# One load for the small inputs, and a new order for the first batch's attention, in a fused attention and squared-ReLU kernel

## The chip, the core and the metric

The kernel runs on one core of a Trainium2 chip. The metric is the device time of one execution in microseconds (us); of the kernel before there are three runs of 1002.27, 1003.53 and 1003.83, median 1003.53. The engines are PE (TensorE, matrix products; its weight loads are a row of their own, PEld), DVE (VectorE), ACT (ScalarE), POOL (GpSimd) and SP (SyncE, which here only issues transfers). A transfer (DMA) can also be issued by ACT.

## What is computed

Eight batches of attention with 12 heads, 448 tokens and 64 columns a head, whose output feeds a two-matrix network with a gate:

```python
q_n, k_n = rmsnorm(q, g_q), rmsnorm(k, g_k)         # over the 64 columns
attn = softmax(q_n @ k_n.T / 8)                     # 448 x 448 a head
x = (attn @ v) put side by side over the heads      # 448 x 768 a batch
xk = mu_k * x + (1 - mu_k) * x_prev                 # x_prev: the token before
xr = mu_r * x + (1 - mu_r) * x_prev
k2 = maximum(xk @ w_k, 0) ** 2                      # w_k 768 x 1024
out = sigmoid(xr @ w_r) * (k2 @ w_v)                # w_r 768 x 768, w_v 1024 x 768
```

g_q and g_k have 64 numbers each, mu_k and mu_r 768 each.

## The kernel before

**Who sets the order.** The program is a set of Python generators (`setup`, `load`, `stats`, `preps`, `vpreps`, `scores`, `attends`, `mixk`, `wload`, `weights`, `moe` and more), each of which yields its next instruction. A planner (`Plan.run`) keeps an estimated clock for each engine and always emits the instruction with the smallest key: the time at which it could start, less a priority times `PS` = 0.1, so that a priority of 700 is worth 70 ns. The order emitted is fixed when the program is built; on the chip each engine works through its own list from the top, and an instruction that waits holds up everything behind it on that engine. Nearly all instructions are emitted in one helper line, L289 in the profile (L290 in the changed kernel), so groups are told apart by the tiles that they write and read.

**Attention.** Two heads are a pair, two pairs a quad; a batch has six pairs, three quads and 21 score groups. For the first batch (quads 0 to 2, `u < U32`) everything is in float32: q and k are scaled (`nat<-qk,ss`), turned by PE transposes (`ps<-ident,nat`), copied to `stk`, and multiplied (`ps<-stk`, 448 columns, one matmul a head and group). DVE takes the row maxima (`sums<-ps`), ACT the exponential with its row sums (`xk<-ps,sums` or `nat<-ps,sums`), POOL divides, PE turns the result back (`ps<-ident,nat` or `ps<-ident,xk`; `xk` here is only memory that is lent out), and DVE or ACT copies it to `pT`. That last part is the function `probs_pe`. When all groups of a pair are there, `attends` multiplies by v (`ps<-pT,vf`, 16 matmuls) and writes the pair's columns of x. From the second batch on the numbers are split into a high and a low half of 16 bits: three products a score group (`ps<-stk` in f16), the exponentials in place (`ps<-ps,sums`), the split (`nat<-ps,sums`), transposes by DMA (`pT<-nat`), and 22 matmuls for a pair's product with v (`ps<-pT,vh` and `ps<-pT,vl`).

**The network.** For each batch `mixk` builds xk from x: per 128 columns one ACT instruction (`ps<-x,bsc`), one on DVE (`df<-x,bsc,ps`), an ACT cast (`xk<-df`) and a POOL subtraction (`xk<-df,xk`); six such pieces make a batch. Then `moe` multiplies: 144 matmuls `ps<-xk,wk`, then 126 `ps<-wr,xr` and 168 `ps<-wv,kk` in turns, and ACT applies the gate (`o<-ps,bsc`). The gate's scale (`bsc`) needs the scales of all weights (`WIN`), so all weights must have been split first.

**Weights.** They arrive as 64-bit numbers in pieces (`raw`, `kk`), are reduced to 32 bits by POOL, ACT (`ps<-raw`) and DVE (`wk<-ps,wk`, and the like), squared and summed on PE (`ps<-wk`, `ps<-wr`, `ps<-wv`, bf16), and split in two halves on ACT and DVE or POOL. Their priority grows with the planner's time against `W_GAP` for each finished piece.

**The small inputs.** `setup` loads g_q and g_k by two transfers from SP that spread one row over 128 partitions. DVE then makes one scaled vector of them and a handful of factors (`gm`, `gc`), some 16 tiny instructions that depend on each other; every scaling of q and k needs `gm`. `mu_stats` loads mu_k and mu_r by two transfers from ACT, once the second quad is being loaded and a piece of weights is there; each puts 768 numbers of 4 bytes on 128 partitions, six a partition, one by one. DVE computes 1 - mu and the largest factor from them.

The lines that set the order here are, in `scores` and `probs_pe`:

```python
yield from until(lambda: u in TQ and len(banks["sc"].free) > (SC_KEEP if u < U32 or gi in PE_P else 1) and not st["zq"])
```

`TQ` holds the quads whose q and k are turned, and `banks["sc"].free` counts the PSUM banks that score groups may still take. Nothing else keeps the second batch's score groups back.

Of the kernel before, what the change touches and what calls it, by code (L numbers as in the profile page):

```python
# [7 lines left out]
F32 = mybir.dt.float32  # L8
# [8 lines left out]
P = 128  # L17
HD = 64
NT = 7
# [3 lines left out]
ND = D_MODEL // P  # L23
# [40 lines left out]
PRIO_M = 400  # L64
BOOST_K = 500
BOOST_R = 500
BOOST_A = 0
BOOST_W = 300
BOOST_Q = 600
SLACK_S = 3  # L70
# [8 lines left out]
Q_DVE = 1  # L79
V_POOL = True  # L80
PE_T = 6
U32 = 3
V_SIDE = 2
SWITCH = 600
# [7 lines left out]
LEAD_V = 1  # L92
LEAD_W = 1
PE_P = range(1, 21, 2)
SC_KEEP = 2
TR_COST = 130
W_GAP = 7e3
W_PUSH = 0.03
NEWTON_ON = "DVE"
OP_SLOW = 1.0  # L100
# [353 lines left out]
            yield V.scalar_tensor_tensor(out=y, in0=t, scalar=1.5, in1=y, op0=ALU.add, op1=ALU.mult)  # L454


def attn_moe_kernel(tc, q, k, v, g_q, g_k, mu_k, mu_r, w_k, w_v, w_r, out):
    nc = tc.nc
    B, H = 2 * out.shape[0], D_MODEL // HD
    NP = H // 2  # L460
# [1 line left out]
    const = ctx.enter_context(tc.tile_pool(name="const", bufs=1))  # L462
    small = ctx.enter_context(tc.tile_pool(name="small", bufs=3))
# [7 lines left out]
    T, V, A, G_, SP = (Engine(n, e) for n, e in (("PE", nc.tensor), ("DVE", nc.vector), ("ACT", nc.scalar), ("POOL", nc.gpsimd), ("SP", nc.sync)))  # L471
# [1 line left out]
    banks = {n: Share(psum, *c) for n, c in (("sc", SC_SHARE), ("mm", MM_SHARE), ("ot", OT_SHARE), ("wz", WZ_SHARE), ("pg", PG_SHARE), ("df", DF_SHARE))}  # L473

    ident16 = const.tile([P, P], BF16, name="ident16")
    gq = const.tile([P, HD], F32, name="gq")
    gk = const.tile([P, HD], F32, name="gk")
    mu = const.tile([P, 2, 2, ND], F32, name="mu")
    gm = const.tile([P, 8], F32, name="gm")
    G = gq  # L480
    gc = const.tile([P, 1], F32, name="gc")
# [14 lines left out]
    NQ, NPAIR, NSS, NSL, NVB = len(quads), len(pairs), 4 * NT, (NT + 1) // 2, 2 * NT  # L496
    VFREE = [const.tile([P, NVB, HD], F32, name="vf%d" % n) for n in range(VF_BUFS)]

    st = {"wdone": 0, "g": 0, "moe": 0, "vl": 0, "gm": False, "mus": False, "want": "xk", "sg": 0, "su": 0, "pu": 0, "vi": 0, "wkeys": 0, "kdone": 0, "zq": 0, "tq": 0, "lu": 0}
    LD, SS, VF, VV, TQ, PT, BS, BSC, XT, XK, XKN, XR, CNT, OS, CARRY, FR = {}, {}, {}, {}, {}, {}, {}, {}, {}, {}, {}, {}, {}, {}, {}, {}  # L500

    plan.st = st
# [1 line left out]
    def until(f):  # L504
        while not f():
            yield f
# [33 lines left out]
    for name, plan_ in (("kk", KK_LENT), ("xk", XK_LENT)):  # L540
        for _ in R[name].get():
            pass
        t = HOME[name] = next(iter(R[name].of.values()))[2]
        w = t.rearrange("p a b c -> p (a b c)")
# [20 lines left out]
    ring_sum = [small.tile([P, 12], F32, name="sums%d" % n, bufs=1) for n in range(6)]  # L565

    def setup():
        yield SP.dma_start(out=gq, in_=g_q.partition_broadcast(P))
        yield SP.dma_start(out=gk, in_=g_k.partition_broadcast(P))
        yield A.copy(out=ident16, in_=ident)  # L570
        yield V.memset(out=ones, value=1.0)
        st["vf"] = True
        yield V.scalar_tensor_tensor(out=G, in0=gq, scalar=1.0 / float(HD) ** 0.5, in1=gk, op0=ALU.mult, op1=ALU.mult)
        yield V.tensor_reduce(out=gm[:, 0:1], in_=G, axis=AX.X, op=ALU.max, apply_absolute_value=True)
        yield V.tensor_scalar(out=gm[:, 0:1], in0=gm[:, 0:1], scalar1=TINY, scalar2=None, op0=ALU.max)
        yield from rsqrt(V, gm[:, 1:2], gm[:, 0:1], gm[:, 5:6])
        yield V.tensor_scalar(out=G, in0=G, scalar1=gm[:, 1:2], scalar2=None, op0=ALU.mult)
        for h in range(2):
            hs = slice(h * HD, (h + 1) * HD)
            yield V.tensor_tensor(out=gd[hs, :], in0=G[hs, :], in1=ident[hs, hs], op=ALU.mult)  # L580
        yield V.tensor_reduce(out=gc, in_=gd, axis=AX.X, op=ALU.add)
        yield V.tensor_tensor(out=gm[:, 2:3], in0=gm[:, 1:2], in1=gm[:, 1:2], op=ALU.mult)
        yield V.tensor_scalar(out=gm[:, 3:4], in0=gm[:, 2:3], scalar1=1.0 / HD, scalar2=None, op0=ALU.mult)
        yield V.tensor_scalar(out=gm[:, 4:5], in0=gm[:, 2:3], scalar1=1e-6, scalar2=None, op0=ALU.mult)
        st["gm"] = True

    def mu_stats():
        yield from until(lambda: st["lu"] >= 1 and len(RAW))
        yield A.dma_start(out=mu[:, 0, 0, :], in_=mu_k.rearrange("(t p) -> p t", p=P))
        yield A.dma_start(out=mu[:, 1, 0, :], in_=mu_r.rearrange("(t p) -> p t", p=P))  # L590
        yield V.tensor_scalar(out=mu[:, :, 1, :], in0=mu[:, :, 0, :], scalar1=-1.0, scalar2=1.0, op0=ALU.mult, op1=ALU.add)
        u = small.tile([P, 2, ND], F32, name="muu")
        u2 = small.tile([P, 2, ND], F32, name="muu2")
        col = small.tile([P, 2], F32, name="mucol")
        yield V.tensor_scalar(out=u, in0=mu[:, :, 0, :], scalar1=2.0, scalar2=-1.0, op0=ALU.mult, op1=ALU.add)
        yield V.tensor_scalar(out=u2, in0=u, scalar1=-1.0, scalar2=1.0, op0=ALU.mult, op1=ALU.max)
        yield V.tensor_tensor(out=u, in0=u, in1=u2, op=ALU.max)
        yield V.tensor_reduce(out=col, in_=u, axis=AX.X, op=ALU.max)
        pt = yield from banks["ot"].get()
        yield T.transpose(form=("f", 200), out=pt[0:2, 0:P], in_=col, identity=ident)  # L600
        m = small.tile([P, 1], F32, name="allmax")
        yield V.tensor_reduce(out=m[0:2, :], in_=pt[0:2, 0:P], axis=AX.X, op=ALU.max)
        yield T.matmul(form=("f", 400), out=pt[:, P:P + 2], lhsT=m[0:2, :].broadcast_to([2, P]), rhs=ident[0:2, 0:2], start=True, stop=True)
        yield V.tensor_copy(out=smu, in_=pt[:, P:P + 2])
        banks["ot"].put(pt)
        yield V.reciprocal(out=ismu, in_=smu)
        st["mus"] = True
# [191 lines left out]

    def scores():  # L800
        for gi, (u, x, t0) in enumerate(groups):
            yield from until(lambda: u in TQ and len(banks["sc"].free) > (SC_KEEP if u < U32 or gi in PE_P else 1) and not st["zq"])
            tp = None
            if u < U32 or gi in PE_P:
# [77 lines left out]
    def probs_pe(u, x, t0, sums, tp):  # L882
# [8 lines left out]
        for a0 in range(0, NT, 4):  # L891
            m = min(4, NT - a0)
            st["zq"] += 1
            z = yield from banks["sc"].get()
            st["zq"] -= 1
            yield [T.transpose(form=("tr", TR_COST * m), out=z[:, a * P:(a + 1) * P], in_=tf[:, (a0 + a) * P:(a0 + a + 1) * P], identity=ident) for a in range(m)]
            src = z[:, 0:m * P].rearrange("p (a c) -> p a c", c=P)
            if u < U32:
                dst = whole(PTQ[:, :, :])[:, a0:a0 + m, c0:c0 + P]
                yield A.copy(out=dst, in_=src) if plan.pick("ACT", "DVE") == "ACT" else V.tensor_copy(out=dst, in_=src)  # L900
            else:
                hi, lo = (PTQ[:, h + a0:h + a0 + m, c0:c0 + P] for h in (0, NT))
                yield A.copy(out=hi, in_=src)
                yield V.tensor_tensor(out=lo, in0=src, in1=hi, op=ALU.subtract)
            banks["sc"].put(z)
        R["nat"].put(tp)
        for i in (2 * u, 2 * u + 1) if t0 == NT - 1 else (2 * u + x,):
            CNT[i] += 1
# [288 lines left out]
    ctx.close()  # L1197


_INS = ["q", "k", "v", "g_q", "g_k", "moe_mu_k", "moe_mu_r", "moe_w_k", "moe_w_v", "moe_w_r"]  # L1200


def layouts(inputs):
# [31 lines left out]
    for name in ("moe_w_k", "moe_w_v", "moe_w_r"):  # L1235
        w = np.asarray(inputs[name])
        a = w.reshape(2, -1, P, w.shape[1] // P, P).transpose(3, 0, 2, 1, 4)
        laid[name] = np.ascontiguousarray(a).reshape(*a.shape[:3], -1)
    return {**laid, "q": qd, "k": kd, "v": vd.reshape(b * h // 2, P, 2 * NT * HD)}


def tokens_back(o, b):
# [29 lines left out]
```

## Time and profile before

| | |
|---|---|
| median of three runs | 1003.53 us |
| the profiled execution | 1002.68 us |
| its span, first to last instruction | 1000.9 us |
| PE busy in the span | 911.1 us, 91% |
| ACT, POOL, DVE busy | 781.2, 675.9, 663.7 us |
| mean granted PE clock | 0.973 |

The span lies 1.78 us under the execution's own time, and that execution 0.85 us under the median. A stage of the kernel shows in the profile as a stretch: the first batch's attention and the weights take the first 157 us, the first batch's network and what there is of the second batch's attention the next 116, and from there on attention and network run side by side until attention ends at about 850 us. Busy shares over the whole span hide that; so the table by stretches, the timeline of the first 25 us and the instructions at the borders of the stages are what is read below.

### The profile page before, as it was taken

What the parts mean: (1) busy time and instruction counts of PE and PEld (TensorE: products, weight loads), DVE (VectorE), ACT (ScalarE), POOL (GpSimd) and SP (SyncE); (2) the same over time, 40 slices, a digit from 0 to 9 for tenths busy, and PEclk for the clock granted to TensorE, in tenths of its full rate; (3) what the DMA queues carried; (4) which work ended last, traced back from release to release, by engine and by line L of the source; (5) the groups of instructions that cost most, each with busy time, mean ns of one, the idle gap of its engine ahead of it and who ended that gap; (6) DMA issues with size and microseconds to landing.
All of it is one profiled execution on the core that took longest, in us unless ns stands there. A gap on an engine that the chain in (4) does not pass through costs nothing. (4 is left out here: it accounts for less than half of the span.)

```text
span 1000.9 us, 18138 instructions
## 1 busy us (share of the span) xinstructions
PE 911.1 (91%) x6048; PEld 478.5 (48%) x6048; DVE 663.7 (66%) x1816; ACT 781.2 (78%) x1740; POOL 675.9 (68%) x744
## 2 busy tenths in 40 slices
PE   0687859799899999999999999989998999999998
PEld 0443434355444555445444555445544555565564
DVE  4797887778875887688875878777866875012000
ACT  2587889889997999999997999999889977424200
POOL 2578898957797777978797777968588624635400
PEclk9798969989999999999999999999999999999999
DMA  5444566499978999799988999999977992100000
GB/s 191 150 153 126 174 183 131 79 200 187 231 145 170 223 215 225 155 205 210 232 168 157 219 208 224 187 185 196 217 170 150 182 182 69 37 16 32 1 33 31
DMA packets 359357, 156.38 MB, mean 156 GB/s; under 512 B 338272, under 2 KB 338272, under 8 KB 359264
## 3 DMA queue, kind: packets, MB, share of 16 engines
q1 hardware_dynamic: 357552, 154.76, 70.5%
q8 instruction: 47, 0.77, 0.3%
q10 hardware_dynamic: 1712, 0.47, 0.2%
q14 instruction: 46, 0.38, 0.1%
HBM read 60.23 MB, written 11.01 MB: 71 GB/s over the span
## 5 line engine op out<-in xcount | busy, mean ns | idle before, releaser
L289 PE MATMUL ps<-wv,kk 128*128 128x384 f16 x1344 | 233.8, 326 | 1.4 <-DVE df L289 1.4
L289 PE MATMUL ps<-xk,wk 128*128 128x448 f16 x1152 | 226.1, 353 | 2.8 <-DVE nat L289 2.2
L289 DVE TENSOR_REDUCE sums<-ps 128x1 f32<-128x448 f32 x336 | 192.3, 613 | 20.4 <-PE ps L289 20.2
L289 ACT ACTIVATE ps<-ps,sums 128x448 f32<-128x448 f32 x294 | 189.3, 646 | 18.3 <-DVE sums L289 16.7
L289 DVE SCALAR_TENSOR_TENSOR nat<-ps,sums,nat 128x448 f16<-128x448 f32 x242 | 158.7, 677 | 56.3 <-ACT nat L289 55.8
L289 ACT ACTIVATE nat<-ps,sums 128x448 f16<-128x448 f32 (+1 forms) x274 | 173.1, 679 | 22.6 <-DVE sums L289 15.0
L289 PE MATMUL ps<-wr,xr 128*128 128x384 f16 x1008 | 180.3, 330 | 2.4 <-DVE o L289 1.3
L289 PEld LDWEIGHTS <-kk 128*128 128x128 f16 (+1 forms) x1350 | 128.0, 98 | 97.6 <-issue 17.1
L289 PEld LDWEIGHTS <-wk 128*128 128x128 f16 (+1 forms) x1194 | 113.4, 99 | 113.5 <-issue 14.2
L289 PE MATMUL ps<-stk 64*128 64x448 f16 (+3 forms) x1104 | 131.5, 384 | 22.0 <-DVE nat L289 9.4
L289 PEld LDWEIGHTS <-xr 128*128 128x128 f16 x1008 | 96.8, 99 | 76.5 <-issue 16.6
L289 DVE SCALAR_TENSOR_TENSOR o<-o,ps 128x384 f32<-128x384 f32 x56 | 30.7, 548 | 108.5 <-PE ps L289 108.3
L289 DVE SCALAR_TENSOR_TENSOR df<-x,bsc,ps 128x448 f32<-128x448 f32 x96 | 63.8, 674 | 54.1 <-ACT ps L289 46.6
L289 PE MATMUL ps<-pT,vh 128*64 128x448 f16 x588 | 93.2, 361 | 0.2
L289 ACT ACTIVATE o<-ps,bsc 128x384 f32<-128x384 f32 x48 | 28.9, 603 | 76.5 <-PE ps L289 76.5
L289 POOL TENSOR_TENSOR qk<-qk,ss 128x896 f32<-128x896 f32 x36 | 60.9, 1693 | 19.1 <-DVE ss L289 15.9
L289 PEld LDWEIGHTS <-stk 64*128 64x128 f16 x1008 | 35.7, 97 | 76.4 <-issue 50.0
L289 POOL TENSOR_SCALAR o<-o,bsc 128x768 f32<-128x768 f32 x24 | 21.8, 910 | 71.7 <-DVE o L289 54.3
L289 POOL TENSOR_TENSOR nat<-nat 128x448 f32<-128x448 f32 x38 | 43.1, 1135 | 38.7 <-ACT nat L289 19.9
L289 ACT ACTIVATE ps<-x,bsc 128x448 f32<-128x448 f32 x96 | 64.4, 683 | 0.8 <-DVE nat L289 0.7
L289 POOL TENSOR_TENSOR xr<-df,xr 128x448 f16<-128x448 f32 x48 | 49.5, 1042 | 21.8 <-ACT xr L289 21.7
L289 POOL TENSOR_SCALAR vf<-vf,bstat 128x896 f32<-128x896 f32 x42 | 42.8, 1019 | 28.2 <-DVE bstat L289 16.3
(172 smaller groups left out, 1553.2 us busy)
## 6 DMA issues: line engine op xcount, KB each, us to landing
vf<-in_v_dram SPq DMA_DIRECT2D x42, 448.0 KB, 4.2
out_dram<-o SPq DMA_DIRECT2D x28, 384.0 KB, 2.8
qk<-in_k_dram SPq DMA_DIRECT2D x23, 448.0 KB, 4.4
qk<-in_q_dram SPq DMA_DIRECT2D x22, 448.0 KB, 4.3
raw<-in_moe_w_v_dram SPq DMA_DIRECT2D x12, 512.0 KB, 3.9
raw<-in_moe_w_r_dram SPq DMA_DIRECT2D x12, 384.0 KB, 3.2
kk<-in_moe_w_k_dram SPq DMA_DIRECT2D x8, 384.0 KB, 3.3
raw<-in_moe_w_k_dram SPq DMA_DIRECT2D x8, 384.0 KB, 3.2
```

What stands on the lines that cost most here:

```text
L289: r = op.fn(op.kw["out"], op.kw["value"]) if op.fn.__name__ == "memset" else op.fn(**op.kw)
```

## The change

The host now lays g_q, g_k, mu_k and mu_r into one array of 128 rows and 152 columns: g_q and g_k repeated on each row, mu with the six numbers that each partition needs. One transfer from SP loads it into one tile, `few`, of which `gq`, `gk` and `mu` are parts. `mu_stats` waits for `gm` instead of for the loads, and has no transfer of its own. In `scores`, groups from the second batch on (`gi` of 21 and more) wait until `probs_pe` has ended for all 21 groups of the first batch, which the new counter `pz` tells. Three numbers of the planner change: attention products get a priority 700 higher while the network waits for xk (`BOOST_A`), a score group of the first batch leaves one PSUM bank free instead of two (`SC_KEEP`), and weights are due every 6 us instead of every 7 (`W_GAP`).

```diff
-BOOST_A = 0
+BOOST_A = 700
...
+AHEAD = 0
...
-SC_KEEP = 2
+SC_KEEP = 1
...
-W_GAP = 7e3
+W_GAP = 6e3
...
-def attn_moe_kernel(tc, q, k, v, g_q, g_k, mu_k, mu_r, w_k, w_v, w_r, out):
+def attn_moe_kernel(tc, q, k, v, small_in, w_k, w_v, w_r, out):
...
-    gq = const.tile([P, HD], F32, name="gq")
-    gk = const.tile([P, HD], F32, name="gk")
-    mu = const.tile([P, 2, 2, ND], F32, name="mu")
+    few = const.tile([P, 2 * HD + 4 * ND], F32, name="few")
+    gq, gk = few[:, 0:HD], few[:, HD:2 * HD]
+    mu = few[:, 2 * HD:].rearrange("p (w a t) -> p w a t", w=2, a=2)
...
     def setup():
-        yield SP.dma_start(out=gq, in_=g_q.partition_broadcast(P))
-        yield SP.dma_start(out=gk, in_=g_k.partition_broadcast(P))
+        yield SP.dma_start(out=few, in_=small_in)
...
     def mu_stats():
-        yield from until(lambda: st["lu"] >= 1 and len(RAW))
-        yield A.dma_start(out=mu[:, 0, 0, :], in_=mu_k.rearrange("(t p) -> p t", p=P))
-        yield A.dma_start(out=mu[:, 1, 0, :], in_=mu_r.rearrange("(t p) -> p t", p=P))
+        yield from until(lambda: st["gm"])
...
     def scores():
         for gi, (u, x, t0) in enumerate(groups):
+            yield from until(lambda: gi < 7 * U32 + AHEAD or st["pz"] == 7 * U32)
...
             banks["sc"].put(z)
+        st["pz"] += 1
         R["nat"].put(tp)
```

**The start of DVE's list.** Rows name the operation, the tile written, the tiles read and the shape. `gm` and `gc` are the factors from g, `muu` belongs to mu, `sst` are the sums of squares of k (`xk`) and q (`nat`). Before:

```order
L289 TENSOR_REDUCE sst<-nat_136 128x14
L289 SCALAR_TENSOR_TENSOR gm<-gm 128x1
L289 TENSOR_SCALAR mu<-mu 128x2x6
L289 SCALAR_TENSOR_TENSOR gm<-gm 128x1
L289 TENSOR_SCALAR muu<-mu 128x12
L289 TENSOR_SCALAR gq<-gq,gm 128x64
L289 TENSOR_SCALAR muu_156<-muu 128x12
L289 TENSOR_TENSOR gk<-gq,ident 64x64 x2
L289 TENSOR_TENSOR muu<-muu,muu_156 128x12
L289 TENSOR_REDUCE gc<-gk 128x1
```

Now:

```order
L290 SCALAR_TENSOR_TENSOR gm<-gm 128x1 x2
L290 TENSOR_SCALAR few<-few,gm 128x64
L290 TENSOR_TENSOR few<-few,ident 64x64 x2
L290 TENSOR_REDUCE gc<-few 128x1
L290 TENSOR_TENSOR gm<-gm 128x1
L290 TENSOR_REDUCE sst<-xk_99 128x14
L290 TENSOR_SCALAR gm<-gm 128x1 x2
L290 TENSOR_SCALAR few<-few 128x2x6
L290 TENSOR_SCALAR muu<-few 128x12
L290 TENSOR_SCALAR muu_152<-muu 128x12
L290 TENSOR_TENSOR muu<-muu,muu_152 128x12
L290 TENSOR_REDUCE sst<-nat_144 128x14
```

The first instruction on mu stood in the middle of the chain for `gm`, ahead of its last row; now that chain and `gc` are complete before the first instruction on mu, and all of it but the last reduction is ahead of q's sums.

**PE where the first f16 score group of the second batch stands.** `ps_1255`, `ps_1279` and `ps_1309` are banks that take turned probabilities of the first batch, `stk_882` and `stk_855` the second batch's first turned quad. Before:

```order
L289 MATMUL ps_1255<-ident,xk_101 128x128 x3
L289 MATMUL ps_1279<-ident,nat_1199 128x128 x4
L289 MATMUL ps_1309<-ident,nat_1199 128x128 x3
L289 LDWEIGHTS stk_882
L289 MATMUL ps_1329<-stk_882 128x448
L289 LDWEIGHTS stk_882
L289 MATMUL ps_1328<-stk_882 128x448
```

Now:

```order
L290 MATMUL ps_1291<-wv 128x128
L290 LDWEIGHTS wv
L290 MATMUL ps_1291<-wv 128x128
L290 MATMUL ps_1334<-ident,nat_1191 128x128 x3
L290 LDWEIGHTS stk_855
L290 MATMUL ps_1345<-stk_855 128x448
L290 LDWEIGHTS stk_855
L290 MATMUL ps_1344<-stk_855 128x448
```

Before, two groups of the first batch (14 transposes) and its last attention product still came behind the second batch's first scores; now `ps_1334` takes the very last transposes of the first batch. PE's first `ps<-xk,wk` stood behind four score groups of the second batch and all squares of wv, and now stands behind three groups and four of the six pieces of wv.

**ACT before the sixth cast of the first batch's xk**, with which that batch's xk is complete. Names as above; `vh` belongs to v. Before:

```order
L289 ACTIVATE nat_1513<-ps_1328,sums_105 128x448
L289 ACTIVATE nat_1513<-ps_1329,sums_105 128x448
L289 ACTIVATE nat_1514<-ps_1341,sums_106 128x448
L289 ACTIVATE nat_1514<-ps_1342,sums_106 128x448
L289 ACTIVATE x_1496<-ps_1497 128x64
L289 ACTIVATE x_1496<-ps_1497 128x384
L289 ACTIVATE ps_1544<-raw_1493 128x512
L289 ACTIVATE ps_1563<-raw_1503 128x512
L289 ACTIVATE ps_1559<-x_1496,bsc 128x448
L289 CAST stk_1326<-ps_1524 128x512
L289 ACTIVATE ps_1532<-ps_1532,sums_107 128x448
L289 CAST xk_101<-df_1558 128x448
```

Now:

```order
L290 CAST xk_99<-df_1400 128x448
L290 ACTIVATE ps_1395<-ps_1395,sums_104 128x448
L290 ACTIVATE wr<-wr,WSC 128x768
L290 ACTIVATE ps_1459<-x_1346,bsc 128x448
L290 ACTIVATE ps_1396,ps_1395<-ps_1396,sums_104 128x448
L290 ACTIVATE nat_1378<-ps_1345,sums_103 128x448
L290 ACTIVATE ps_1443<-ps_1443,sums_105 128x448
L290 ACTIVATE ps_1470<-raw_1435 128x512
L290 CAST wr<-wr 128x768
L290 CAST xk_99<-df_1458 128x448
```

The sixth cast was ACT's instruction 187 and is now 173: work on weights and on the second batch has moved behind it. The last split of the weights (`wv<-wf,WSC`) moved back in ACT's list from row 225 to row 253, and the first gate (`o<-ps,bsc`) stands at row 266 in both.

More of the change, by code (lines that the diff above doesn't have):

```diff
@@ L497, in attn_moe_kernel @@
     VFREE = [const.tile([P, NVB, HD], F32, name="vf%d" % n) for n in range(VF_BUFS)]
-    st = {"wdone": 0, "g": 0, "moe": 0, "vl": 0, "gm": False, "mus": False, "want": "xk", "sg": 0, "su": 0, "pu": 0, "vi": 0, "wkeys": 0, "kdone": 0, "zq": 0, "tq": 0, "lu": 0}
+    st = {"wdone": 0, "g": 0, "moe": 0, "vl": 0, "gm": False, "mus": False, "want": "xk", "sg": 0, "su": 0, "pu": 0, "vi": 0, "wkeys": 0, "kdone": 0, "zq": 0, "tq": 0, "lu": 0, "pz": 0}
     LD, SS, VF, VV, TQ, PT, BS, BSC, XT, XK, XKN, XR, CNT, OS, CARRY, FR = {}, {}, {}, {}, {}, {}, {}, {}, {}, {}, {}, {}, {}, {}, {}, {}
@@ L1197, in attn_moe_kernel @@
     ctx.close()
-_INS = ["q", "k", "v", "g_q", "g_k", "moe_mu_k", "moe_mu_r", "moe_w_k", "moe_w_v", "moe_w_r"]
+_INS = ["q", "k", "v", "small", "moe_w_k", "moe_w_v", "moe_w_r"]
 def layouts(inputs):
@@ L1238, in layouts @@
         laid[name] = np.ascontiguousarray(a).reshape(*a.shape[:3], -1)
-    return {**laid, "q": qd, "k": kd, "v": vd.reshape(b * h // 2, P, 2 * NT * HD)}
+    few = np.zeros((P, 2 * HD + 4 * ND), np.float32)
+    few[:, 0:HD], few[:, HD:2 * HD] = inputs["g_q"], inputs["g_k"]
+    for w, name in enumerate(("moe_mu_k", "moe_mu_r")):
+        o = 2 * HD + 2 * ND * w
+        few[:, o:o + ND] = np.asarray(inputs[name]).reshape(ND, P).T
+    return {**laid, "small": few, "q": qd, "k": kd, "v": vd.reshape(b * h // 2, P, 2 * NT * HD)}
 def tokens_back(o, b):
```

## The prediction

> **What bounds the kernel now.** The first view is the table by stretches, whose borders I put at the first products of the network; each row gives a stretch's length and each engine's busy time in it. Beside it stand the two longest pieces of the chain of waits.
>
> ```profile
> core 0: us, PE busy (x) PEld busy (x) DVE busy (x) ACT busy (x) POOL busy (x), PEclk, DMA share, GB/s
> 0.00:13.00 13.00, 0.37 (x2) 0.21 (x2) 4.80 (x16) 5.73 (x10) 3.99 (x10) 1.00 0.69 230
> 13.00:25.00 12.00, 1.39 (x6) 1.10 (x7) 6.29 (x31) 0.00 (x0) 1.07 (x3) 1.00 0.42 150
> 25.00:130.00 105.00, 80.77 (x475) 44.60 (x475) 87.64 (x236) 76.03 (x177) 77.45 (x104) 0.90 0.47 149
> 130.00:157.30 27.30, 16.16 (x107) 8.38 (x104) 21.96 (x44) 25.55 (x53) 23.85 (x27) 0.69 0.71 209
> 157.30:206.10 48.80, 40.92 (x247) 19.76 (x247) 37.65 (x91) 43.98 (x94) 42.68 (x42) 0.90 0.53 101
> 206.10:272.90 66.80, 63.67 (x466) 33.68 (x465) 54.75 (x157) 61.37 (x141) 44.52 (x46) 1.00 0.98 204
> 272.90:761.50 488.60, 473.42 (x3277) 240.74 (x3278) 372.78 (x1057) 456.14 (x1032) 385.51 (x401) 1.00 0.95 194
> 761.50:996.00 234.50, 234.39 (x1479) 130.00 (x1478) 77.25 (x189) 112.41 (x238) 95.90 (x115) 0.99 0.33 71
> ```
>
> ```profile
> 761.51 15.60 PE ps L289 x95
> 777.12 206.86 PE ps L289 x1311
> ```
>
> Length less PE's busy time is PE's idle time: 12.6, 10.6, 24.2, 11.1, 7.9, 3.1, 15.2 and 0.1, together 84.8 us. From 761.5 on PE never waits, and the chain is PE alone; from 206 on it idles 18.4 us in 790. So the end is PE's work plus PE's idle time, and 66.5 of the 84.8 us lie ahead of 206. PE's instructions are the same in number and kind after the change, so the time can only move by PE's idle time (and the clock). In the early stretches PE isn't what limits: in 25 to 130 DVE is the busiest (87.6 of 105), from 130 to 157 ACT (25.55 of 27.3), and from there to 761 ACT is at 90 to 93%.
>
> The second view is the timeline of the start, with the transfers' landing times (last column, us).
>
> ```profile
> 0.73 0.41 ACTq L289 DMA_DIRECT2D xk<-in_k_dram  x1
> 6.82 0.87 ACTq L289 DMA_DIRECT2D mu<-in_moe_mu_r_dram  x1
> 7.92 0.67 DVE L289 SCALAR_TENSOR_TENSOR gq<-gq,gk 128x64 f32<-128x64 f32 x1 [7.05 <-DMA gk<-in_g_k_dram]
> 8.97 0.95 ACT L289 ACTIVATE nat<-xk 128x896 f32<-128x896 f32 x1 [1.66 <-DMA xk<-in_q_dram]
> 12.24 0.61 DVE L289 TENSOR_REDUCE sst<-nat 128x14 f32<-128x448 f32 x1
> 12.77 0.26 DVE L289 SCALAR_TENSOR_TENSOR gm<-gm 128x1 f32<-128x1 f32 x1
> 18.24 0.17 DVE L289 TENSOR_SCALAR mu<-mu 128x12 f32<-128x12 f32 x1 [5.22 <-DMA mu<-in_moe_mu_r_dram]
> 19.82 0.17 DVE L289 TENSOR_SCALAR ps<-sst 128x14 f32<-128x14 f32 x1
> 22.84 1.09 DVE L289 TENSOR_TENSOR nat<-xk,ss 128x896 f32<-128x896 f32 x1
> ```
>
> ```profile
> gq<-in_g_q_dram SPq DMA_DIRECT2D x1, 32.0 KB, 4.7
> gk<-in_g_k_dram SPq DMA_DIRECT2D x1, 32.0 KB, 6.6
> mu<-in_moe_mu_r_dram ACTq DMA_DIRECT2D x1, 3.0 KB, 11.4
> ```
>
> DVE stands still for 5.22 us because the first instruction on mu waits for 3 KB that take 11.4 us to land. Behind it in DVE's list are the end of the `gm` chain and the scaling of q and k, without which PE has nothing to turn; ACT starts no instruction at all from 13 to 25.
>
> **The start.** The two loads of mu go, and the one load that takes their place is the first on SP. DVE's stall of 5.22 us goes with certainty if that load lands before 12.8: it starts at about 0.74 like g_q's, which landed in 4.7 us, so at about 5.5. The `gm` chain can then start at 5.5 instead of 7.92, and its end (the small instructions between 18.32 and 19.82) moves ahead of q's sums. What is then left is q itself: its sums end at 12.85 now, the chain `ps<-sst` to `nat<-xk,ss` takes 22.84 - 19.82 = 3.0 us, and the four small instructions on mu, 0.17 each, stand between. That makes 12.85 + 0.7 + 3.0 = 16.5 in place of 22.84: 6.3 us at most. One thing works against it: in ACT's list k's load now stands behind the table load and a cast instead of at 0.73, about 1.6 us later; but k's squares were done well before q's (8.97), so 1 us of it at most can show. Bounds 5.2 and 6.3; I take 6, as the row of the stall is the nearest.
>
> **The first batch's end.** ACT's sixth cast of xk was its instruction 187 and is now 173. By my count of the whole order list the difference is five `ps<-raw`, two `nat<-qk`, two `stk<-ps,gc`, two f16 splits and one split of wr. The means in the stretch 25 to 157.3 (busy us, then mean ns):
>
> ```profile
> L289 ACT ACTIVATE nat<-qk 128x896 f32<-128x896 f32 x9 | 8.5, 958 | 0.0
> L289 ACT ACTIVATE ps<-raw 128x512 f32<-128x512 f32 x12 | 7.6, 638 | 0.7 <-DVE wv L289 0.7
> L289 ACT ACTIVATE stk<-ps,gc 128x512 f32<-128x512 f32 x3 | 2.1, 688 | 17.6 <-PE ps L289 17.6
> L289 ACT ACTIVATE nat<-ps,sums 128x448 f16<-128x448 f32 x4 | 2.2, 636 | 0.3 <-DVE sums L289 0.3
> L289 ACT ACTIVATE wr<-wr,WSC 128x768 f16<-128x768 f32 x2 | 1.9, 936 | 1.2 <-POOL wr L289 1.1
> ```
>
> 5 x 0.638 + 2 x 0.958 + 2 x 0.688 + 2 x 0.636 + 0.936 = 8.7 us, and some 8 since each starts about 0.1 us before the last one's end. So the first `ps<-xk,wk`, at 157.35, should come at about 157.35 - 6 - 8 = 143. That alone is no gain: nothing was taken away, only put behind.
>
> **What was put behind comes due at the first gate.** The rows at the next borders:
>
> ```profile
> 157.35 2.43 PE L289 MATMUL ps<-xk,wk 128*128 128x448 f16 x12
> 182.03 1.21 ACT L289 ACTIVATE wv<-wf,WSC 128x1024 f16<-128x1024 f32 x1
> 199.73 0.51 POOL L289 TENSOR_SCALAR bsc<-WIN,bsc 128x1 f32<-128x1 f32 x2
> 206.15 2.11 PE L289 MATMUL ps<-wr,xr 128*128 128x384 f16 x12
> 210.06 0.58 ACT L289 ACTIVATE o<-ps,bsc 128x384 f32<-128x384 f32 x1 [1.89 <-PE ps L289]
> 270.94 1.12 ACT L289 CAST xk<-df 128x448 f16<-128x448 f32 x2
> 272.88 7.38 PE L289 MATMUL ps<-xk,wk 128*128 128x448 f16 x38 [1.51 <-DVE nat L289]
> ```
>
> The first gate is ACT's row 266 in both orders, with the same instructions ahead within 0.2 us. ACT can reach it earlier only by idling less: by the start's 6, and by part of the 4.8 us that it idles in 157.3 to 206.1, of which 1.89 is a wait for PE. PE's work ahead of its first `ps<-wr,xr` is the same too, less four transposes. So there the gain is 6 to 10.8; I take 7.5, the start and the larger part of the wait for PE.
>
> **The second batch's xk.** Ahead of that batch's sixth cast ACT has three instructions more, 1.9 us by the same count. In 206.1 to 272.9 ACT idles 5.4 of 66.8, so PE, which waited there 1.51 us, will again be held by it: 272.9 - 7.5 + 1.9 = 267.3. In that time PE has done more: ahead of that product its list has one attention product of 22 matmuls (2.2 us) and one score group (0.74) more, 3.0. PE's idle time up to there was 272.9 - 203.3 = 69.6 and becomes 267.3 - 206.3 = 61.0: **8.6 us less**. Bounds: 5.2 - 1.9 + 3.0 = 6.3 with the stall alone, and 10.8 + 5.4 - 1.9 + 3.0 = 17.3 where ACT never idles.
>
> **The rest.** In 272.9 to 761.5 PE idles 15.2 us. ACT has more ahead of some batches' xk (21.6 us for the fifth, by the count), but reached that cast at 581.6 where PE used it at 616.3, and PE comes only 8.6 earlier; so 581.6 - 6 + 21.6 = 597 against 608. I take nothing for it, and 4 us to either side. `BOOST_A`, `SC_KEEP` and `W_GAP` act through these orders only and have no term of their own. The sum, against the profiled execution: 1002.68 - 8.6 = 994.1. It lies 0.85 under the median shown, so 995.
>
> **A rule that speaks against it.** The granted clock fell where PE had little to do:
>
> ```profile
> 130.00:140.00 10.00, 4.84 (x35) 2.75 (x31) 8.38 (x15) 9.93 (x21) 9.64 (x10) 0.69 0.76 232
> 140.00:150.00 10.00, 5.18 (x22) 2.73 (x23) 7.29 (x15) 9.02 (x19) 9.33 (x11) 0.50 0.58 173
> 195.00:206.10 11.10, 6.88 (x45) 3.03 (x42) 8.59 (x25) 10.30 (x27) 8.73 (x14) 0.54 0.78 164
> ```
>
> The Trainium skill ("TensorE: Matmul & The Clock Gate", "What's actually happening") says that a window of about 3.4 us without enough activity halves PE's clock until a busy window has passed. By that rule, which these rows agree with, holding back score groups thins PE's work in the first batch's stage and could put a half-clock stretch on the network's first products. Priced from the rows: the long one lasted some 17 us (the 0.69 and 0.50 slices); 17 us of products at half speed take 8.5 us more. It would eat the gain.
>
> **The rivals.** (1) *The weights come late, slower.* The last split of wv on ACT has 16.6 us more ahead and comes at 182.0 - 6 + 16.6 = 192.6. Before, the first gate followed it by 28.0 us. If that distance is a chain of dependent work, the gate falls at 220.6, 10.5 us later, and PE, which has two banks for these products, stands: 1013. It decides from the point where split to gate takes over 17.5 us. Against it: of the 28 us only about 8 are instructions of that chain; `bsc<-WIN` at 199.73 waited in POOL's list. (2) *More than forecast.* ACT idles hardly at all from 143 on, toward the bound of 17.3: say 14, so 989 and below. (3) *Swallowed.* PE is ahead of ACT from the third batch on, and what it won early it waits for later; ACT at 93% in 272.9 to 761.5 speaks for it, its 32 us of idle time there against PE's 15 against it: about 1002. (4) *Half clock*, above: about 1003.
>
> **How the numbers follow.** My forecast 0.55; rival 1 0.13, rival 2 0.16, rival 3 0.09, rival 4 0.07. The forecast's own range is 990 to 1000 (6.3 less 4 at the poor end, and half-way to 17.3 at the good one). For eight in ten I go to 986, where rival 2 mostly lies, and to 1003, which takes in rivals 3 and 4; rival 1 and the last of rival 2 are left out. A difference under 0.2%, 2 us, can't be told from none. Faster: the forecast, rival 2 and a little of rival 3, 0.75; no change: most of rivals 3 and 4, 0.11; slower: rival 1 and the rest, 0.14.
>
> **What would show it.** Right: no wait of DVE for a transfer of mu; the first `nat<-xk,ss` at 16 to 18; the first `ps<-xk,wk` near 143, the first gate at 200 to 205, the second batch's `ps<-xk,wk` at 265 to 270; PE idle 74 to 78 us in all. Wrong: the scaling of q still past 20 (another input is late), the first gate past 210 (the weights), a clock below 0.9 in the stretch from the first product to the gate and past it, or PE idle over 20 us between the second batch's xk and the tail.

## The result, and the profile after

The change takes the median from 1002.9 us (four runs of the kernel before, the three above and one more) to **993.36 us** (four runs, 992.15 to 993.59): a ratio of **0.9902**, interval 0.9885 to 0.9919. The forecast was 995. The profiled execution took 993.59 us, its span is 991.8, PE is busy for 913.7 us of it (before 911.1).

The milestones of both profiled executions; in brackets, PE's idle time up to there:

| us | before | after | earlier by |
|---|---|---|---|
| first scaling (`nat<-xk,ss`) | 22.84 | 14.22 | 8.6 |
| first `ps<-xk,wk` | 157.4 (58.6) | 137.2 (44.1) | 20.2 |
| first `ps<-wr,xr` | 206.2 (66.5) | 190.8 (53.0) | 15.4 |
| first gate | 210.06 | 195.73 | 14.3 |
| second batch's `ps<-xk,wk` | 272.9 (69.6) | 263.8 (56.4) | 9.1 |
| last matmul's end | 995.9 (84.8) | 986.7 (73.1) | 9.2 |

The prediction and some expectations call the first scaling that of q. By the kernel's `preps` it is k's, and q's follows at 17.76 in the kernel after. It needs the sums of squares of both, and q's come last, so the argument doesn't hang on the name.

The table by stretches of the kernel after, with borders at the same products (columns as in the prediction):

```profile
core 0: us, PE busy (x) PEld busy (x) DVE busy (x) ACT busy (x) POOL busy (x), PEclk, DMA share, GB/s
0.00:137.20 137.20, 93.11 (x543) 51.22 (x544) 113.48 (x313) 101.40 (x231) 97.78 (x135) 0.88 0.53 170
137.20:190.80 53.60, 44.72 (x285) 22.47 (x283) 40.62 (x84) 49.49 (x103) 49.97 (x51) 0.91 0.61 144
190.80:263.80 73.00, 69.57 (x496) 36.93 (x496) 61.25 (x182) 65.06 (x151) 43.60 (x44) 0.95 0.96 194
263.80:987.00 723.20, 706.25 (x4730) 369.04 (x4728) 450.09 (x1237) 565.40 (x1259) 483.06 (x515) 1.00 0.74 153
```

Length less PE's busy time gives the idle time: 44.1, 8.9, 3.4 and, up to the last matmul's end, 16.7 us. Before, it was 58.6, 7.9, 3.1 and 15.2 for the same stages. All of the saving lies ahead of the first product of the network; from there on PE idles 2.8 us more. The gain made in the first batch shrinks on its way, 20, 15, 9, and what is left at the second batch's xk, 9.1, is there at the end too. In between it isn't the same at every border: the fifth batch's `ps<-xk,wk` comes 3.9 us earlier (612.5 for 616.3).

The timeline of the start of the kernel after (start, length, engine, instruction, idle time before it):

```profile
2.60 0.23 DVE L290 SCALAR_TENSOR_TENSOR few<-few 128x64 f32<-128x64 f32 x1 [1.73 <-DMA few<-in_small_dram]
6.41 0.15 DVE L290 TENSOR_TENSOR gm<-gm 128x1 f32<-128x1 f32 x1
7.51 0.93 ACT L290 ACTIVATE nat<-xk 128x896 f32<-128x896 f32 x1
9.51 0.42 DVE L290 TENSOR_SCALAR few<-few 128x12 f32<-128x12 f32 x1
10.67 0.61 DVE L290 TENSOR_REDUCE sst<-nat 128x14 f32<-128x448 f32 x1
14.22 1.09 DVE L290 TENSOR_TENSOR nat<-xk,ss 128x896 f32<-128x896 f32 x1
```

Its list of transfers (KB, us from issue to landing):

```profile
few<-in_small_dram SPq DMA_DIRECT2D x1, 76.0 KB, 1.8
```

The first instruction on mu, at 9.51, waits for nothing. The `gm` chain begins at 2.60 instead of 7.92, since the 76 KB landed in 1.8 us where g_k's 32 KB had taken 6.6, and q's squares come at 7.51 instead of 8.97.

Between the last split of wv and the first gate, in the timeline of the kernel after:

```profile
182.98 1.21 ACT L290 ACTIVATE wv<-wf,WSC 128x1024 f16<-128x1024 f32 x1
188.16 0.66 POOL L290 TENSOR_SCALAR bsc<-WIN,bsc 128x1 f32<-128x1 f32 x2 [1.53 <-DVE WIN L290]
195.73 0.58 ACT L290 ACTIVATE o<-ps,bsc 128x384 f32<-128x384 f32 x1 [0.96 <-PE ps L290]
```

The split comes 0.95 us later than before, the gate 14.3 us earlier: from split to gate it is 12.75 us, not 28.0. `bsc<-WIN` follows the split by 5.2 us (17.7 before) because POOL now stands waiting for it.

PE's busy time grew by 2.6 us with the same number of matmuls. An estimate of the clock's part: half of PE's busy time in the stretches at a granted clock of 0.5 is lost, which makes 19.5 us in the trace of before and 21.1 in that of after. So some 1.6 of the 2.6 us are clock; for the other 1.0 the runs show no cause. Three pairs of stretches in the kernel after:

```profile
255.50:259.00 3.50, 1.07 (x12) 0.36 (x8) 3.50 (x10) 3.47 (x9) 2.85 (x3) 1.00 1.07 203
259.00:262.50 3.50, 3.08 (x16) 1.31 (x18) 2.81 (x11) 3.50 (x10) 3.50 (x4) 0.51 1.09 253
...
303.50:307.00 3.50, 0.96 (x7) 0.60 (x8) 1.19 (x3) 3.50 (x8) 3.50 (x4) 0.98 1.08 217
307.00:310.50 3.50, 3.50 (x13) 1.72 (x12) 2.42 (x8) 1.92 (x4) 3.50 (x4) 0.53 0.95 228
429.50:433.00 3.50, 1.56 (x11) 0.72 (x10) 0.62 (x1) 1.37 (x3) 3.50 (x5) 1.00 1.12 253
433.00:436.50 3.50, 3.50 (x12) 1.74 (x13) 0.98 (x2) 0.00 (x0) 3.29 (x5) 0.52 1.10 268
```

In each pair, 3.5 us in which PE had 1.0 to 1.6 us of work are followed by 3.5 us at a granted clock near 0.5. Behind 206 us these three places stand here, and two like them before (659 and 762 us). This is the rule that the prediction took from the Trainium skill ("TensorE: Matmul & The Clock Gate", "What's actually happening"), and the trace agrees with it, for windows that were not empty: 3.5 us that are mostly idle cost up to another 1.7 us at half speed.

### The profile page after: what moved, and what is told of

It is laid out like the page before. It is cut to its first block, busy times and chain, and to the rows that moved or that the text cites. A ratio compares the mean times of both kernels' runs of the same rounds, so it can differ in the third digit from the quotient of the medians.

```text
span 991.8 us, 18142 instructions
## 1 busy us (share of the span) xinstructions
PE 913.7 (92%) x6048; PEld 479.7 (48%) x6048; DVE 665.8 (67%) x1815; ACT 781.4 (79%) x1741; POOL 675.3 (68%) x744
## 5 line engine op out<-in xcount | busy, mean ns | idle before, releaser
L290 PE MATMUL ps<-wr,xr 128*128 128x384 f16 x1008 | 182.5, 332 | 3.8 <-ACT x L290 3.3
L290 PEld LDWEIGHTS <-wk 128*128 128x128 f16 (+1 forms) x1194 | 113.6, 99 | 112.0 <-issue 14.9
L290 POOL TENSOR_TENSOR xk<-df,xk 128x448 f16<-128x448 f32 x48 | 49.6, 1036 | 22.2 <-ACT xk L290 22.0
```

Source lines behind the costliest of these rows:

```text
L290: r = op.fn(op.kw["out"], op.kw["value"]) if op.fn.__name__ == "memset" else op.fn(**op.kw)
```

## The experiments

Several theories could stand behind the 9.5 us: the earlier **start** alone; the new **order** alone; within the order, the **hold** on the second batch's scores or the three **numbers** of the planner; and the **plan** as such, meaning that any replanned order lands somewhere in a spread that no part of the change explains. Two kinds of kernel tell them apart. In the first kind every engine's list is kept row for row and only loads or a delay differ. In the second the planner runs anew. Ratios are against the kernel before, run beside each kernel on its chip.

### Lists kept: the one load with the old order

The lists of before; the one transfer is issued in place of g_q's, the other three are not issued.

```diff
+            if op.fn.__name__.startswith("dma") and getattr(op.kw["out"], "tensor", None) is aps(self.few[0]).tensor:
+                if e == "SP" and not self.loaded:
+                    self.loaded = True
...
+                        self.last[e] = op.fn(out=aps(self.few[0]), in_=self.few[1])
+                continue
```

> Every engine's list of instructions is that of the kernel before, row for row; only the four small transfers are replaced by the one of the changed kernel. Theory A (the gain is the start: what DVE no longer waits for at the start comes off the end nearly whole): the stall of 5.22 us at the first instruction on mu is gone and g is there earlier, so the scaling of q starts at 14 to 17 instead of 22.8 and the end comes 5 to 8.5 us earlier: ratio 0.9915 to 0.995. Theory B (the gain is the order: the stages up to the second batch are limited by ACT and DVE further on, and an earlier start is taken up there): less than 2 us, ratio 0.998 or more.

Measured: 993.53 us, **0.9912** [0.9895, 0.9930]. Its table by stretches, borders at the same products:

```profile
0.00:150.10 150.10, 99.89 (x584) 55.20 (x585) 123.02 (x324) 107.65 (x240) 106.18 (x143) 0.87 0.55 174
150.10:199.40 49.30, 42.10 (x247) 19.99 (x246) 38.87 (x91) 43.74 (x94) 42.60 (x42) 0.86 0.47 96
199.40:266.20 66.80, 63.59 (x466) 33.41 (x465) 54.78 (x157) 61.46 (x141) 44.57 (x46) 1.00 0.96 204
266.20:990.00 723.80, 708.81 (x4756) 371.12 (x4756) 451.17 (x1246) 568.72 (x1269) 480.90 (x515) 0.99 0.74 154
```

The first scaling comes at 15.32, 7.5 us earlier than before, and every border comes 6.7 to 7.3 us earlier (150.1 for 157.4, 199.4 for 206.2, 266.2 for 272.9). The last matmul ends 6.6 us earlier, since PE idles 9.9 us less and is busy 3.3 us more; this profiled execution, at 996.14, is the slowest of the six. By the ratio this is nearly the whole gain of the change, without its order.

### Lists kept: the four loads with the new order

The reverse: the lists of after, with g_q and g_k on SP in place of the one load, and the two loads of mu on ACT ahead of its first squares.

```diff
+                for o, i in ((gq, g_q), (gk, g_k)):
...
+                        self.last[e] = op.fn(out=o, in_=i.partition_broadcast(P))
...
+            if e == "ACT" and self.mus and op.fn.__name__ == "activation" and op.kw["func"] == AF.Square:
+                for o, i in self.mus:
...
+                        self.last[e] = self.tc.nc.scalar.dma_start(out=o, in_=i)
```

> The lists of the changed kernel, row for row, but with the four transfers of the kernel before, g_q and g_k from SP at the start and mu_k and mu_r from ACT ahead of k's squares. The first instruction on mu stands behind the whole chain for gm here, but still ahead of q's sums, so DVE stalls there until mu lands at about 18. Theory A: the start is as late as before, the gain is at most the 1 to 3 us that the order brings: 1000 to 1002, ratio 0.997 to 0.999. Theory B: the order keeps most of the gain: 994 to 996, ratio 0.991 to 0.993.

Measured: 997.67 us, **0.9946** [0.9927, 0.9965]. Its timeline of the start:

```profile
14.42 0.17 DVE L301 TENSOR_SCALAR few<-few 128x12 f32<-128x12 f32 x1 [1.47 <-DMA few<-in_moe_mu_r_dram]
18.89 1.09 DVE L301 TENSOR_TENSOR nat<-xk,ss 128x896 f32<-128x896 f32 x1
```

The run was not as clean as meant. Issued ahead of k's squares, mu lands by 14.42 instead of 18.24, so that the start is still 3.9 us earlier than before's, and the time lies between what the two theories expected. By what the next run shows of such a shift, 3.9 us are worth 3.4 to 4.2 at the end; of the 5.4 us measured, 1 to 2 are left for the order, which is no more than the interval's half width of 1.9.

### Lists kept: the start put back

The change with nine unused reductions on DVE, ahead of the second sums, as a delay.

```diff
+DEAD = 9
...
+                if self.sums == 2:
+                    for _ in range(DEAD):
...
+                            self.last[e] = self.tc.nc.vector.tensor_reduce(out=self.dead[:, 0:7], in_=bcast(self.ident[:, :], 7), axis=AX.X, op=ALU.max)
```

> The changed kernel with its one load, and nine reductions of 896 columns (about 1 us each by the width, 9 us together) put into DVE's list ahead of q's sums, whose result nothing uses; every other row of every list is the changed kernel's. It measures by itself what a late start costs. Theory A: the scaling of q starts at about 23 as in the kernel before and the end comes 7 to 9 us later than the changed kernel's: 1000 to 1002, ratio to the kernel before 0.997 to 0.999. Theory B: the end comes at most 2 us later, ratio 0.990 to 0.993.

Measured: 1002.97 us, **1.0009** [0.9997, 1.0021]. Its timeline shows the delay and the first scaling; below it stands its table by stretches:

```profile
10.62 10.05 DVE L296 TENSOR_REDUCE dead<-ident 128x7 f32<-128x896 f32 x9
24.13 1.09 DVE L298 TENSOR_TENSOR nat<-xk,ss 128x896 f32<-128x896 f32 x1
```

```profile
0.00:146.10 146.10, 90.07 (x544) 47.68 (x545) 121.70 (x322) 101.53 (x231) 97.67 (x135) 0.93 0.50 160
146.10:199.50 53.40, 44.83 (x285) 22.47 (x284) 40.29 (x85) 49.51 (x103) 50.91 (x51) 0.91 0.63 144
199.50:272.60 73.10, 69.40 (x495) 36.97 (x494) 61.45 (x183) 65.39 (x152) 43.93 (x44) 0.95 0.95 194
272.60:995.50 722.90, 705.09 (x4730) 368.60 (x4728) 449.64 (x1237) 564.54 (x1259) 482.79 (x515) 1.00 0.74 153
```

The first scaling comes 9.9 us later than after, and every later border comes 8.5 to 8.9 us later (146.1, 199.5, 272.6; the last matmul ends at 995.2 for 986.7). So 0.85 of the shift reaches the end in the profiled executions, as 12.7 us more of idle PE less 4.3 us of busy PE, and all of it by the two ratios (0.0107 of 1002 us is 10.7 us). The start is 1.3 us later here than before, and the time is before's: with a start as late as that, the order is worth some 1 us at most. The theory that the order alone carries the gain falls, and that of the start holds: with the lists kept, the start moved by itself in either direction takes the end with it.

### Replanned: the loads alone

One load, no hold, the old numbers; the planner makes its order for this.

```diff
-BOOST_A = 700
+BOOST_A = 0
...
-AHEAD = 0
+AHEAD = 1000
...
-SC_KEEP = 1
+SC_KEEP = 2
...
-W_GAP = 6e3
+W_GAP = 7e3
```

> The changed kernel without the hold on the second batch's scores and with the three old numbers of the planner; the one load stays, and the planner knows of it, so that all lists are planned anew behind it. Theory A: like the old order with the new loads, a gain of 5 to 8.5 us, give or take 3 us that any new plan moves the later stages: ratio 0.989 to 0.998. Theory B: the plan without the hold and the numbers gains under 2 us: ratio 0.998 to 1.002.

Measured: 1001.63 us, **0.9989** [0.9975, 1.0003], with the first scaling at 13.60, earlier than in the change itself. That is what theory B expected of it. Three rows of its table by stretches:

```profile
131.00:151.50 20.50, 12.37 (x52) 7.20 (x54) 15.17 (x39) 13.33 (x25) 13.86 (x19) 0.51 0.63 212
151.50:158.00 6.50, 2.43 (x23) 0.94 (x20) 4.62 (x10) 5.59 (x13) 4.41 (x6) 1.00 0.68 170
158.00:171.70 13.70, 9.87 (x41) 4.19 (x42) 10.80 (x26) 11.14 (x25) 9.31 (x9) 0.50 0.55 103
```

PE idles 8.8 us less than before (76.0), but is busy 8.4 us more (919.5): 34 us around the first product run at half clock, and by the estimate above half clock costs 28.0 us in this kernel, against 19.5 before. In this plan the sixth cast of xk is ACT's row 197, against 187 before and 173 after, and the first product comes at 165.9. At the first product nothing is left of the early start: PE has idled 58.7 us by then, against 58.6 before.

### Replanned: the hold and the numbers apart

First the change without the hold, then the hold with the three old numbers.

```diff
-AHEAD = 0
+AHEAD = 1000
```

> The changed kernel with its one load and its three new numbers, without the hold on the second batch's scores; planned anew. Its sixth cast of the first xk is ACT's row 180 (173 in the changed kernel, 197 in the one with the loads alone). Theory C (the hold is what turns the early start into gain under a new plan): most of the gain is lost, 999 to 1002, ratio 0.997 to 1.000. Theory D (the numbers do it): as fast as the changed kernel, ratio 0.989 to 0.992. Theory E (neither; every new plan shifts the time by some us either way): anything between, first product of the network between 137 and 166.

```diff
-BOOST_A = 700
+BOOST_A = 0
...
-SC_KEEP = 1
+SC_KEEP = 2
...
-W_GAP = 6e3
+W_GAP = 7e3
```

> The changed kernel with its one load and the hold, but with the three old numbers; planned anew. Its sixth cast of the first xk is ACT's row 190. Theory C: as fast as the changed kernel, ratio 0.989 to 0.992. Theory D: most of the gain is lost, ratio 0.997 to 1.000. Theory E: anything between.

Measured: without the hold 995.77 us, **0.9941** [0.9923, 0.9959]; the hold with the old numbers 1005.37 us, **1.0033** [1.0020, 1.0047]. The table by stretches of the second, for the stretch between the first `ps<-wr,xr` and the second batch's `ps<-xk,wk`:

```profile
201.50:279.40 77.90, 69.81 (x500) 36.27 (x499) 67.58 (x188) 71.04 (x164) 49.97 (x54) 0.93 1.04 213
```

PE idles 8.1 us here, where it idled 3.1 before and idles 3.4 in the change. That is not what makes it slow, though: in all, this execution idles 5.4 us less than before (79.4 for 84.8) and is busy 4.3 us more, and at 1001.67 it is the fastest of twelve. The longer times of the others go with a lower mean clock, down to 0.959 (0.967 here); no trace shows where it is lost. Neither the hold nor the numbers explain the gain by themselves, as theory E has it. The hold with the old numbers is slower than any theory expected and the slowest of all kernels, though its first scaling comes 9.2 us earlier than before; the numbers without the hold keep 6 us.

### Replanned: a neighbour, and a start made still earlier

A planner's estimate that has nothing to do with the change, the cost of a transpose on PE, raised by 2 ns:

```diff
-TR_COST = 130
+TR_COST = 132
```

> The changed kernel with one estimate of its planner moved by 1.5% (a transpose costs it 132 ns instead of 130). Nothing is meant by it; but nearly half of PE's list comes out in another order. Theories C and D expect the changed kernel's time within 2 us: ratio 0.988 to 0.992. Theory E expects a time as far from it as those of the other new plans, 3 us or more either way.

Measured: 989.47 us, **0.9883** [0.9865, 0.9901]. A change of no meaning moved the ratio by 0.002, where the whole order moved it by 0.001 with the lists kept; but the interval overlaps that of the change, and the time lies where theories C and D expected it, not 3 us away as theory E did. What speaks for E is the estimate of 131 further down, 0.0056 away with intervals that don't touch. PE is idle 66.1 us here, the least of all, and busy 915.8.

Then the change's own lists, with k's load on ACT ahead of the table load and a cast, and the four instructions on mu behind the first scaling:

```diff
+        if e == "ACT" and op.fn.__name__ == "copy" and "ident16" in name:
+            self.kept.append((e, op))
...
+        if e == "DVE" and op.fn.__name__ in ("tensor_scalar", "tensor_tensor") and ("muu" in name or "few" in name and op.kw["out"].ap[-1][1] == ND):
+            self.kept.append((e, op))
```

> The changed kernel's lists with two moves at the start: k's load goes ahead of the table load and the cast in ACT's list, and the four small instructions on mu go behind the scaling of k. If the start goes over into the end as the delayed start did (8.5 us at the end for 9.9 at the start), the scaling starts about 1.2 us earlier, at 13, and the end comes 1 us earlier than the changed kernel's: ratio to the kernel before 0.988 to 0.991. If something else limits the start (q's load), it starts where it does and the time is the same.

Measured: 993.61 us, **0.9925** [0.9908, 0.9941], and the first scaling no earlier. Its timeline and, as the last row, its transfer:

```profile
4.16 0.23 DVE L287 SCALAR_TENSOR_TENSOR few<-few 128x64 f32<-128x64 f32 x1 [3.30 <-DMA few<-in_small_dram]
5.43 1.33 DVE L287 SCALAR_TENSOR_TENSOR gm<-gm 128x1 f32<-128x1 f32 x2
6.77 1.12 POOL L313 TENSOR_TENSOR nat<-nat 128x448 f32<-128x448 f32 x1
6.80 1.11 DVE L287 TENSOR_TENSOR gm<-gm 128x1 f32<-128x1 f32 x1
14.62 1.09 DVE L287 TENSOR_TENSOR nat<-xk,ss 128x896 f32<-128x896 f32 x1
...
few<-in_small_dram SPq DMA_DIRECT2D x1, 76.0 KB, 3.4
```

Side by side with k's 448 KB the small load takes 3.4 us, the `gm` chain begins 1.6 us later, and its tiny instructions then fall into the time of POOL's two adds; one of them stretches to 1.11 us, two to 1.33 together. What was won on k was lost on g.

### Replanned: does a count of the lists rank the plans?

The last four runs test the theory of the plan. A count from the lists, the D of the formula in the expectations, says how far ACT's work ahead of the second batch's sixth cast exceeds PE's work ahead of that batch's first product, with mean durations from the trace of before. A small count should mean little idling. Two plans with a small one and two with a large one were run, all with the one load:

```diff
-TR_COST = 130
+TR_COST = 131
```

> The changed kernel with its planner's estimate for a transpose at 131 ns instead of 130: a new plan. For every plan a number D is counted from its lists with the mean durations of the kernel before: ACT's work ahead of the sixth cast of the second batch's xk, less PE's work ahead of the first product on it. Theory F (D tells what a plan is worth, since PE stands idle as long as ACT's lead in work is long): the five plans run so far with the early start have D of 25.4, 26.5, 28.6, 30.7 and 32.9 us and came out 9.8, 11.7, 5.9 and 1.1 us faster and 3.3 us slower than the kernel before; a straight line through them is -5.0 + 2.0 x (D - 28.8). This plan has D = 23.8: 15 us faster, ratio 0.985. Theory E (a plan's worth can't be told from its list up to there): anywhere from 12 us faster to 3 us slower.

```diff
-W_GAP = 6e3
+W_GAP = 6.5e3
```

> The changed kernel with weights due every 6.5 us instead of every 6: a new plan with D = 24.3. Theory F: 14 us faster than the kernel before, ratio 0.986. Theory E: anywhere from 12 us faster to 3 us slower.

```diff
-BOOST_A = 700
+BOOST_A = 0
```

> The changed kernel with the old number for the priority of the attention products, 0 instead of 700; the hold and the two other numbers stay. A new plan with D = 28.6. Theory F: 5.5 us faster than the kernel before, ratio 0.9945. Theory E: anywhere from 12 us faster to 3 us slower.

```diff
-AHEAD = 0
+AHEAD = 1
```

> The changed kernel, but one score group of the second batch is let through ahead of the hold. A new plan with D = 31.6. Theory F: 0.5 us slower than the kernel before, ratio 1.0005. Theory E: anywhere from 12 us faster to 3 us slower.

| | the count | median us | ratio | PE idle | PE busy |
|---|---|---|---|---|---|
| `W_GAP` 6.5e3 | 24.3 | 985.18 | 0.9829 [0.9815, 0.9842] | 71.0 | 907.2 |
| `TR_COST` 131 | 23.8 | 986.56 | 0.9846 [0.9830, 0.9862] | 70.7 | 909.0 |
| `AHEAD` 1 | 25.4 | 988.79 | 0.9863 [0.9848, 0.9878] | 71.1 | 911.4 |
| `BOOST_A` 0 | 29.9 | 991.92 | 0.9897 [0.9880, 0.9913] | 74.9 | 909.8 |
| the change | 25.4 | 993.36 | 0.9902 [0.9885, 0.9919] | 73.1 | 913.7 |

The two plans with the small counts came out fastest, as expected. The two that were to be slow were not: the counts in their expectations were taken from other lists than those that ran, which have 25.4 and 29.9 (the column above). With these the formula gives -11.8 us for `AHEAD` 1 (measured -13.7) and -2.8 for `BOOST_A` 0 (measured -10.3). It misses the last by over 7 us, and the change itself, with a count equal to that of `AHEAD` 1, is 4 us slower than it. Theory E is no better off: three of the four came out more than its 12 us faster. Over all nine replanned kernels PE's idle time goes up with the count, from 70.7 us at 23.8 to 79.4 at 32.9, but for the plan with 132, which idles least, 66.1, at 26.5. The count ranks plans roughly and doesn't settle one; the line was also drawn through five of the nine.

The fastest, by stretches:

```profile
0.00:134.10 134.10, 90.43 (x535) 49.20 (x536) 110.13 (x305) 98.57 (x225) 95.97 (x133) 0.91 0.53 171
134.10:188.80 54.70, 45.12 (x279) 22.58 (x279) 40.92 (x82) 47.98 (x99) 49.53 (x45) 0.87 0.56 140
188.80:258.70 69.90, 64.54 (x475) 34.80 (x473) 61.41 (x180) 62.86 (x146) 42.55 (x49) 0.99 0.92 183
258.70:979.00 720.30, 707.15 (x4762) 369.64 (x4762) 451.59 (x1251) 573.49 (x1275) 487.12 (x518) 1.00 0.76 156
```

Against the change it idles 2.1 us less in all (71.0 for 73.1) and PE is busy 6.5 us less for the same matmuls, with a mean clock of 0.978 against 0.971. It beats both kernels, with an interval clear of the change's. Half clock costs it 14.9 us by the estimate above, against 21.1, so most of its advantage is clock; why this plan leaves fewer stretches with little work for PE was not tested.

## Why the prediction was right

The sum held: PE idles 11.8 us less, PE's work grew by 2.6, the end is 9.2 earlier, where the forecast had 8.6 and nothing. Its terms held less well: more idle time went than forecast, and the busy time that came made up for part of it, so that 993.4 lies as near to 995 as it does is in part luck. The forecast's own range was also added up with a slip: 6.3 less 4 puts its poor end at 1001, not 1000.

**What bounds the kernel** held: PE's last matmul ends 5.0 us ahead of the span's end before and 5.1 after, so the sum of its busy and its idle time tells the time. The prediction set PE's work as constant; over the 14 kernels it went from 907.2 to 919.5 us. By the estimate above 14.9 to 28.0 us of it are half clock and the rest lies between 891 and 895, so the clock is no smaller an unknown than the idle time.

**The start** was too small: 8.6 us, not 6, above the upper bound of 6.3. That bound took the end of q's sums, 12.85, as set by q alone. POOL's add ahead of these sums, before and after:

```profile
9.99 1.13 POOL L289 TENSOR_TENSOR nat<-nat 128x448 f32<-128x448 f32 x1 [1.49 <-ACT nat L289]
8.78 1.13 POOL L290 TENSOR_TENSOR nat<-nat 128x448 f32<-128x448 f32 x1
```

Before, the add ended at 11.12, but DVE was still in the `gm` chain and began the sums at 12.24. That chain now is, but for two instructions, through at 6.6, ahead of POOL's adds (from 7.69), because `few` took 1.8 us to land and not the 4.7 of g_q's row: 1.12 us. And the add ends 1.21 us earlier, since q's load was issued at 1.19 instead of 1.66 and its squares started 1.46 us earlier. The two make up the 2.3 us above the bound. What was to work against it was small: k's load was issued 0.6 us later, not 1.6. The mechanism, a stall of DVE on 3 KB in the middle of a chain, was right: the run with the old order and the new load shows it alone.

**The first batch's end** was forecast at 143 and came at 137.2, 20 us earlier for a sum of 14. That this "alone is no gain" is confirmed: against the old order with the new load, the new one brings the first product forward by 12.9 us, the gate by 7.6, the second batch's xk by 2.4, and the time by 0.001 of the ratio, inside the intervals of both.

**The first gate** came 14.3 us earlier, not 7.5, and above the bound of 10.8. The work ahead of it on ACT was the same, so all of it is idle time of ACT that went. The bound added the stretch behind the first product to the start, and nothing came from there (ACT idles 4.1 us in it, 4.8 before). It came from ahead of the first product: 50.0 us of idle time before, 42.5 with the old order and the new load, 35.8 after. So half of it is the start and half the order, which keeps ACT busier while the first batch ends; the prediction had held that part at nothing.

**The second batch's xk** was forecast at 267.3 with 61.0 us of idle time, and came at 263.8 with 56.4: 13.2 less, between the 8.6 taken and the bound of 17.3. PE had been busy 4.1 us more by then (207.4 for 203.3), where the sum had 3.0 us of further work; half clock is in these 4.1 too, and the term for ACT's three further instructions was not measured apart.

**The rest** was set at 0, within 4: behind the second batch's xk PE idles 16.7 us instead of 15.2. What the prediction did not have in the sum is PE's busy time: 2.6 us more, some 1.6 of it by the clock.

**What would show it**: DVE waits for no transfer of mu, as said. The numbers were all missed on the good side: the first scaling at 14.22 for 16 to 18, the first product at 137.2 for 143, the gate at 195.7 for 200 to 205, the second batch's xk at 263.8 for 265 to 270, 73.1 us of idle time for 74 to 78. Only the time lay inside; without the 2.6 us of busy PE it would have been some 991, at the edge of the forecast's range.

**The rivals.** Weights late: the last split came at 182.98, not at 192.6, and the distance from it to the gate was not all a chain of work: some 12.5 of its 28.0 us were a wait in POOL's list (`bsc<-WIN` followed the split by 17.7 us, and now by 5.2), as the argument against this rival said. It shrank to 12.75 us, below the 17.5 from which it would have decided. More than forecast: in idle time up to the second batch's xk yes (13.2 near its 14), in the end no (9.2), and not by its mechanism: ACT idles 12.0 us between the first product and the second batch's xk, more than the 10.3 before, and the time was won ahead of the first product. Swallowed: no. A shift of the start reaches the end at 0.85 or more; of what the order gained, PE's idle time was 4.2 us less at the second batch's xk (56.4 against 60.6) and 1.8 at the end (73.1 against 74.9), so a part of the order's gain was swallowed. Half clock: here it took some 1.6 us; in the replanned loads alone it took 8.4 of 8.8, near the 8.5 that the prediction had priced, and cancelled the gain.

What the prediction lacked is the spread of plans. With nearly the same start (13.4 to 14.2), replanned lists went from 0.9829 to 1.0033, some 20 us, and 1 ns in one estimate alone made 5.6 of them. Where in this spread the change's own plan would lie, the sixth of nine, its terms could not tell. What makes a plan good stays open: all plans that had the hold and at least two of the three new numbers gained 10 to 17 us, but the old `W_GAP` and `SC_KEEP` were not tried apart.

## What to carry to other kernels

A small, slow transfer that is read in the middle of a chain of dependent instructions stalls all that stands behind it, and where the later lists are fixed, most of that stall (0.85 and more here) reaches the end even 970 us later: lay such inputs out for the partitions and look at the first 25 us. Work put behind a border shows as a large gain at that border and comes due at the next, so read a new order at the second and third border. And before an order is credited with a gain, run the rest of the change with the old lists row for row; replanning by itself moved the time by up to 5.6 us for 1 ns in an estimate, and over nine plans the times spread by 20 us. Trying a few neighbouring plans found more than the change's own order did.

## What the runs showed of the hardware

**Landing times.** 3 KB in elements of 4 bytes landed in 8.0 to 12.1 us over two kernels; 76 KB in rows of 608 bytes took 1.8 to 2.0 us over ten kernels as the first transfer with k's load 0.6 us behind it, 3.4 and 4.1 when k's load started beside it.

**Tiny DVE instructions beside POOL.** Instructions on one element a partition take 0.15 to 0.18 us each; while POOL's add of 448 columns ran, one took 1.11, ending with POOL's add (6.80 + 1.11 and 6.77 + 1.12). The Trainium skill ("SBUF — State Buffer", "SBUF: two separate sides") says that a DVE instruction with two inputs in SBUF and a POOL instruction that reads SBUF exclude each other for a whole instruction; the rows agree for this instruction, which has two inputs.

**The clock.** 3.5 us with 1.0 to 1.6 us of matmuls were enough for the next 3.5 us to run at half clock, also in the middle of stretches in which PE is 95% busy and more (69.6 of 73.0 us, 706.3 of 723.2). Over the 14 kernels PE's busy time spread by 12 us with the same 6048 matmuls, and what half clock costs, by the estimate above, by 13.
